# Lightweight convolution and SiLU layer on one core: exponents clamped on ScalarE, and one block's taps issued ahead of another's matmuls

## The chip, the core and the metric

One core of a Trainium2 chip runs the whole program. The metric is the device time in microseconds (us); lower is better. Three runs of the kernel before give 2204.98, 2205.42 and 2208.08 us, median 2205.42. The engines are TensorE (PE; its weight loads are PEld), VectorE (DVE), ScalarE (ACT), GpSimd (POOL) and SyncE (SP, which here issues most DMAs). Each works through its own queue in order.

## What is computed

`x` is 8 x 4096 x 192 (32768 rows of 192 channels), fp32. `weight` is 8 x 7; `w_in` is 192 x 2048, `w_out` 2048 x 192.

```python
w = softmax(weight, axis=-1)                  # 8 heads x 7 taps, each head has 24 channels
x_pad = 6 rows of zeros ahead of each of the 8 sequences
y[b, s, h, g] = sum_k w[h, k] * x_pad[b, s + k, h, g]
h = y.reshape(32768, 192) @ w_in
g = h * (1 / (1 + exp(-h)))
out = g @ w_out                               # float32
```

## The kernel before

**Blocks.** The 32768 rows go in 32 blocks of 1024 (`TT`). For each block: x is loaded (`load`, token `ld`), transposed on VectorE (`turn_in`, `i`), given a halo of six columns (`halo_in`, `ha`), and the seven taps are applied (`conv`, `v`): tap 0 on ScalarE, taps 1 to 6 as one multiply-add each on VectorE. Each block has a wide part of 1024 columns (`v.00` to `v.06`) and a narrow one of 512 (`v.10` to `v.16`). The result is split into a high part (`hx`), a low part (`lx`) and a difference (`dx`, moved by DMA in `dm`). Then come the h matmuls (`up`, tokens A, B, C, E), a scaling in place (X), the Silu on ScalarE (S), sums of g on VectorE (`s..`), and the down projection of the *previous* block (Q, D), its store (`st`).

**The order.** Nothing is left to a scheduler: `pin` keeps every engine's instructions in the order in which the program issues them, and from block 1 on that order is the string `PLAN` (lines 63 to 87), walked by the loop at line 852. A token with `-` belongs to the block before, one with `+` to the next; `step` (614) issues a token once and skips it ever after. Token T (line 518) is a copy of one column of a PSUM bank into the tile `dot` on VectorE. It reads the second bank of a pair of h banks, so the next matmul that writes this bank must wait for it. In `PLAN`, `C.00 A.000 T.00 A.010 C.01 T.01 A.001`: A.001 writes the bank that T.00 reads.

**The weights.** The inputs `w_in` and `w_out` come as 64-bit words and are rounded to fp32 in integer arithmetic. That is a `Unit` (line 306): units 0 to 7 are `w_in` (part 0, 512 columns, and part 1, 256 columns, for each of four j), units 8 to 11 are `w_out` (768 columns). For a unit,

- `exponent` masks the exponent bits on VectorE, then clamps and rescales them in two operations, on VectorE for units 0 and 8 (`late` is false there) and on GpSimd for the other ten;
- `sign` (ScalarE) turns the lowest byte into a sticky bit; `mantissa` and `sticky` are VectorE;
- `rounded` is three VectorE operations: the first needs mantissa and sticky, the second the clamped exponent, the third writes the weights to `wd`;
- `top` (ScalarE) makes the high part; `split` makes a low part with a subtraction on VectorE, copies it on ScalarE and makes a third part on VectorE. The low part stands in one buffer for all units of part 0 and one for all of part 1;
- `spread` sends halves of part 1 to the other 64 partitions by DMA.

`begin` (649) issues exponent and sign; `work` (655) is a generator of two pieces: begin of the next unit, mantissa and sticky; then rounded, top and spread.

**Block 0** (lines 762 to 839) runs on plain fp32 while the weights become ready. TensorE convolves its 128 first channels itself (`conv_on_pe`), ScalarE copies the four results (`conv_taken`) to `x_first[0]`; the other 64 channels are convolved by `conv(0, 1, i)`. `up_both(0)` and `up_first(j, c0)` are its h matmuls, each ended by four Silus on ScalarE for a set of four banks; `up_first` takes 128-row matmuls in one turn and 64-row ones in the other. The first h matmul needs unit 0, the first 64-row one needs unit 1 and all taps, `j` needs units 2j and 2j + 1. `woven` (676) interleaves these with the pieces of units 2 to 9 by hand-given costs, which decides the order in ScalarE's queue. Around the up matmuls that order reads: sign 7, top 6, four Silus, copy of split 2, sign 8, top 7, four Silus, copies of splits 5, 4, 7, 6.

Behind them (lines 812 to 831): loads of block 1, units 10 and 11, block 1's transposes, eight of the sums in `combine_out`, its taps, its high and low parts, block 2's loads, block 1's differences, block 2's transposes. Then block 0's plain down projection on TensorE (192 matmuls), and the loop over `PLAN` from block 1 on, in which block 2's taps stand as `+v..` between block 1's matmuls.

Of the kernel before, what the change touches and what calls it, by code (L numbers as in the profile page):

```python
# [8 lines left out]
F32 = mybir.dt.float32  # L9
# [3 lines left out]
AF = mybir.ActivationFunctionType  # L13
ALU = mybir.AluOpType
# [4 lines left out]
def kernel(  # L19
# [18 lines left out]
    H, K = weight.shape  # L38
    NT = B * S
    DFF = moe_w_in.shape[1]  # L40
    P = 128
# [8 lines left out]
    NJ = NCH // 4  # L50
    SQ = 32
    HT = TB // 2
    SPLIT = 4096.0
    assert D == NK * R == H * grp and NK == 3 and S % TT == 0 and DFF == 4 * P * NJ

    x_w = x.flatten_outer_dims().rearrange("(b k t) d -> b t k d", k=TT // SQ, t=SQ)
# [3 lines left out]
    const = ctx.enter_context(tc.tile_pool(name="const", bufs=1))  # L60
# [74 lines left out]
    class Pinned:  # L135
        def __init__(self, engine):
            self.engine = engine
# [4 lines left out]
    vec, act, pool = Pinned(nc.vector), Pinned(nc.scalar), Pinned(nc.gpsimd)  # L142
    sync = Pinned(nc.sync)

    def flat(t):
        names = "abcd"[: len(t.shape) - 1]
        return t.rearrange(f"p {' '.join(names)} -> p ({' '.join(names)})")
# [4 lines left out]
    def f32(t):  # L152
        return t.bitcast(F32)
# [63 lines left out]

    NG = D // SQ
    room = flat(g_all[:, 0, 0])
    used = [0]  # L220

    def early(n):
        used[0] += n
        return room[:, used[0] - n : used[0]]

    w32 = early(SQ)
# [16 lines left out]
    warm = early(1)  # L243
    vec.memset(zeros, 0.0)
    vec.memset(warm, 0.0)
    act.activation(warm, warm, AF.Exp)

    one_hot = early(R)
# [30 lines left out]
    def raw(key):  # L279
        if RAW[key] is None:  # L280
            return flat(g_all[:, 1, 8:11]).bitcast(I32)[:, WC : 3 * WC]
        return flat(RAW[key]).bitcast(I32)[:, 0 : 2 * WC]
# [10 lines left out]
    def load_out(q, queue):  # L293
        queue.dma_start(out=raw(("o", q)).rearrange("p (c d) -> p c d", c=4), in_=out32[q])
# [2 lines left out]
    LOW = CA + CB  # L297
    spare = flat(g_all[:, 1, 8:11])
    low_all, sticky_out = spare[:, 0:LOW], spare[:, LOW + 2 * WC : 2 * LOW + 2 * WC]
    ONE = 1 << 20  # L300
    NEW_SLOTS = 8
    BELOW = 1.0 - 2.0**-13

# [2 lines left out]
    class Unit:  # L306


        def __init__(self, index, key, part):
            j = key[1]  # L310
            self.key, self.part, self.j, self.late = key, part, j, index > 0
            lo, hi = {0: (0, CA), 1: (CA, WC), None: (0, WC)}[part]
            n = hi - lo
            words = raw(key)[:, 2 * lo : 2 * hi]
            pairs = words.rearrange("p (c t) -> p c t", t=2)
            self.lo, self.hi = pairs[:, :, 0], pairs[:, :, 1]
            self.byte = words.bitcast(U8).rearrange("p (c t) -> p c t", t=8)[:, :, 0]
            at_ = scratch[:, 2 * WC * (index % 2) : 2 * WC * (index % 2) + 2 * WC]
            self.ex = at_[:, 0:n].bitcast(I32)
            self.mh = at_[:, n : 2 * n].bitcast(I32)  # L320
            if part is None:
                self.w = wd[:, j, 0:12, :].rearrange("p (a s) d -> p (a s d)", a=2)
                self.st = sticky_out.bitcast(I32)
            else:
                self.low = low_all[:, CA * part : CA * part + n]
                self.st = self.low.bitcast(I32)
            if part is not None:
                at_c = slice(0, 4) if part == 0 else slice(0, 2)
                self.to = [flat(w[:, j, at_c, :]) for w in ws[part]]
                self.w = flat(w_in[part][:, j, at_c, :])  # L330

        def exponent(self):
            vec.tensor_single_scalar(self.ex, self.hi, 0x7FF * ONE, op=ALU.bitwise_and)
            engine = pool if self.late else vec
            engine.tensor_scalar(
                self.ex, self.ex, scalar1=float(896 * ONE), scalar2=float(1151 * ONE), op0=ALU.max, op1=ALU.min
            )
            engine.tensor_scalar(
                self.ex, self.ex, scalar1=float(896 * ONE), scalar2=8.0, op0=ALU.subtract, op1=ALU.mult
            )  # L340

        def sign(self):
            act.activation(self.st, self.byte, AF.Sign)
# [1 line left out]
        def mantissa(self):  # L345
            vec.tensor_scalar(
                self.mh, self.hi, scalar1=ONE - 1, scalar2=ONE, op0=ALU.bitwise_and, op1=ALU.bitwise_or
            )
# [21 lines left out]
        def split(self):  # L370
            vec.tensor_tensor(self.low, self.w, f32(self.to[0]), op=ALU.subtract)
            act.activation(self.to[1], self.low, AF.Copy, scale=SPLIT)
            vec.scalar_tensor_tensor(
                out=self.to[2], in0=f32(self.to[0]), scalar=1.0 / SPLIT, in1=self.low, op0=ALU.mult, op1=ALU.subtract
            )
# [20 lines left out]
    def heat(times):  # L396
        for _ in range(times):
            pin(
                nc.tensor.matmul(
                    banks[5][:, 0 : 2 * P],  # L400
                    zeros,
                    zeros.unsqueeze(1).to_broadcast([P, 2, P]),
                    start=True,
                    stop=True,
                )
            )
# [11 lines left out]
    by_channel = early(D)  # L418
    top, total, part_ = (wred[:, i : i + 1] for i in range(3))
    heat(7)  # L420
    for q in range(1, 4):
        vec.tensor_copy(w32[SQ * q : SQ * q + H, 0:K], w32[0:H, 0:K])
    vec.tensor_reduce(top, logits, axis=AX.X, op=ALU.max, negate=True)
    act.activation(logits, logits, AF.Exp, bias=top, accum_out=total)
    for i in (1, 3):
# [39 lines left out]
    def conv(b, k, i):  # L465
        n = (TT, TB)[k]
        src, dst, tap = xts[k][:, i : i + n], flat(nats[k]), taps[:, k, i : i + 1]
        if i == 0:
            act.activation(dst, src, AF.Copy, scale=tap)
        else:  # L470
            vec.scalar_tensor_tensor(
                out=dst, in0=src, scalar=tap, in1=dst, op0=ALU.mult, op1=ALU.add
            )

    def split(b, k, what):
# [6 lines left out]
        else:  # L482
            vec.scalar_tensor_tensor(
                out=di if k else d_room(b), in0=f32(lo), scalar=SPLIT, in1=f32(hi), op0=ALU.mult, op1=ALU.subtract
            )

    def d_room(b):

        return flat(g_all[:, 1, 8]) if b == 1 else flat(nats[0])
# [12 lines left out]
    def up(b, what, j, c, n=0):  # L502
# [16 lines left out]
        elif what == "X":  # L519
            to = at(b, names[n])  # L520
            if f"X.{j}{c}{n}" in ON_DVE:
                vec.tensor_scalar(to, to, scalar1=1.0 + 1.0 / SPLIT, scalar2=None, op0=ALU.mult)
            else:
                act.activation(to, to, AF.Copy, scale=1.0 + 1.0 / SPLIT)
        else:
# [118 lines left out]
    units = [Unit(2 * j + i, ("i", j), i) for j in range(NJ) for i in range(2)]  # L644
# [4 lines left out]
    def begin(u):  # L649
        if u < len(units):  # L650
            units[u].exponent()
            if u <= 2 * NJ:
                units[u].sign()

    def work(u):

        now = units[u]
        if u > 1:
            begin(u + 1)
        now.mantissa()  # L660
        now.sticky()
        if 2 * NJ < u + 1 < len(units):
            units[u + 1].sign()
        yield
        if not u:
            begin(1)
        now.rounded()
        if now.part is not None:
            if u:
                now.top()  # L670
            now.spread(w_in[1][:, now.j, :, :])
        if u in LATER:
            load_out(LATER[u], sync)
        yield
# [33 lines left out]
    def conv_taken(q):  # L708
        act.copy(x_first[0][:, ts(q, HT)], banks[q][:, 0:HT])

    def drain(stream):
        for _ in stream:
            pass

    def pieces(stream, *costs):
        def one():
            next(stream, None)

        return [(one, cost) for cost in costs]

    def pieces_of_work(u):
        return pieces(work(u), *((26, 30) if u >= 2 * NJ else (14, 13) if u % 2 else (16, 21)))

    x_first = [flat(nats[k]) for k in range(2)]

# [42 lines left out]
    turn_first(True)  # L768
    conv_on_pe(1)
    begin(0)  # L770
    first_ = [work(u) for u in range(2)]
    next(first_[0])
    for q in (0, 2):
# [3 lines left out]
    for q in range(4):  # L777
        at_ = slice(SQ * q, SQ * q + SQ)
        pool.tensor_copy(taps[at_, 1, :], taps_all[at_, 4 + q % 2, 0:K])
        pool.tensor_copy(taps[at_, 0, :], taps_all[at_, ORDER[q], 0:K])  # L780
    conv(0, 1, 0)
    next(first_[0])
    for q in (1, 3):
        conv_taken(q)
    units[0].top()
    conv(0, 1, 1)
    for stream in first_:
        drain(stream)
    begin(2)
    for i in range(2, K):  # L790
        conv(0, 1, i)
    for part in (0, 1):
        load_in(3, part, sync)
# [4 lines left out]
    turns = ["ha.0", "i.0", "ha.1", "i.1", "ha.2"]  # L798
    convs = [t for t in rest_of if t.split(".")[0] == "v"]
    rest = []  # L800
    SPLIT_AFTER = {3: (1,), 4: (0,), 5: (3,), 6: (2,), 7: (5, 4, 7, 6)}
    for u in range(2, 2 * NJ):
        rest += pieces_of_work(u)
        rest += [(units[v].split, 8 if v % 2 else 14) for v in SPLIT_AFTER.get(u, ())]
    for u in (2 * NJ, 2 * NJ + 1):
        rest += pieces_of_work(u)
# [7 lines left out]
    for u in (2 * NJ + 2, 2 * NJ + 3):  # L814
        drain(work(u))
# [8 lines left out]
        step(2, t)  # L824
    for t in ("dx.0", "dx.1", "dm.0"):
        step(1, t)
    for t in turns:
        step(2, t)
    for t in plan:
        if t[0] == "*":  # L830
# [21 lines left out]
    for b in range(1, NB + 3):  # L852
        for t in plan:
            if b == 2 and t[:2] == "-Q":
                drain(late)
            name = t[1:] if t[0] in BACK else t
# [44 lines left out]
```

## Time and profile before

| what | us |
|---|---|
| median of three runs (lowest, highest) | 2205.42 (2204.98, 2208.08) |
| the profiled execution, device time | 2204.53 |
| its span, first to last instruction | 2202.7 |
| TensorE busy in the span | 2192.1 |
| VectorE, ScalarE, GpSimd busy | 1868.1, 1218.8, 52.3 |
| first h matmul of block 0, of block 1, of block 2 starts at | 14.37, 99.93, 169.46 |

The granted TensorE clock is 0.999 over the span. Times of rows below count from the first instruction. A timeline row gives start, length, engine, line, operation, out<-in, the shape and how many instructions were merged in it; in brackets, the idle time of the engine before it and what ended it. Nearly all instructions carry line 140 (the wrapper that pins them), matmuls line 498, so the tiles tell what a row is: `wd` takes rounded weights, `nat` with `taps` is a tap, `xt<-nat` a transpose, `dot` is token T, `g<-ps` a Silu, `xs` the split parts of x.

### The profile page before, as it was taken

How to read it: one execution, taken by the hardware profiler on the slowest of the kernel's cores; microseconds unless marked ns; L12 is line 12 of the kernel's file. 1: busy time of each engine (PE TensorE's matmuls, PEld its weight loads, DVE VectorE, ACT ScalarE, POOL GpSimd, SP SyncE). 2: the span in 40 equal slices, each digit the busy share in tenths (PEclk: the TensorE clock that was granted, in tenths of full speed). 3: DMA queues.
4: the chain of work that ended last, by engine and by line, in shares of the span. 5: the costliest groups of instructions: out<-in, count | busy, mean ns of one | idle time of the engine just before them, and what ended most of it. 6: DMA issues, size and time to landing. Idle time of an engine off the chain costs nothing.

```text
span 2202.7 us, 46351 instructions
## 1 busy us (share of the span) xinstructions
PE 2192.1 (100%) x19294; PEld 1585.3 (72%) x19294; DVE 1868.1 (85%) x2723; ACT 1218.8 (55%) x2457; POOL 52.3 (2%) x75
## 2 busy tenths in 40 slices
PE   9999999999999999999999999999999999999998
PEld 4477777777777777777777777777777777777776
DVE  8898888888888888888888888888888888888867
ACT  5356654466544566545665446664456654466543
POOL 4300000000000000000000000000000000000000
PEclk9999999999999999999999999999999999999999
DMA  6412022220122210222201222112222022221112
GB/s 160 80 25 36 7 37 39 40 39 15 26 39 39 39 30 11 39 40 40 39 13 28 39 39 39 24 17 40 39 39 38 8 34 40 40 39 20 21 25 49
DMA packets 416579, 80.10 MB, mean 36 GB/s; under 512 B 402544, under 2 KB 406640, under 8 KB 416368
## 3 DMA queue, kind: packets, MB, share of 16 engines
q1 hardware_dynamic: 411760, 75.42, 18.7%
q8 instruction: 151, 2.47, 0.5%
q0 software_dynamic: 288, 1.05, 0.3%
q10 hardware_dynamic: 4320, 0.66, 0.2%
q14 instruction: 60, 0.49, 0.1%
HBM read 31.47 MB, written 25.17 MB: 26 GB/s over the span
## 4 chain that ended last, share of the span: by engine, by line
PE 95%; DVE 1%; SPq 0%; ACT 0%; issue 0%; DMA 0%; DVEq 0%
PE ps L498 95%; DVE nat L140 1%; SPq L140 0%; DVE wd L140 0%; DVE fin L140 0%; DMA xs<-g 0%; DVE xt L140 0%; ACT nat L140 0%; ACT fin L140 0%; DVE xs L140 0%; ACT ps L140 0%; DVEq L140 0%; DVE dot L140 0%
## 5 line engine op out<-in xcount | busy, mean ns | idle before, releaser
L498 PE MATMUL ps<-g,wd 128*64 128x256 f32 (+1 forms) x10112 | 1118.8, 383 | 0.0
L498 PEld LDWEIGHTS ps<-g,wd 128*64 128x64 f32 x10112 | 723.5, 137 | 392.0 <-issue 26.7
L140 DVE TENSOR_TENSOR g<-g 128x1024 f32<-128x1024 f32 (+1 forms) x811 | 945.5, 1210 | 21.2 <-PE ps L498 11.3
L140 ACT ACTIVATE ps<-ps 128x512 f32<-128x512 f32 (+1 forms) x961 | 499.4, 581 | 421.7 <-PE ps L498 387.3
L140 ACT ACTIVATE g<-ps 128x512 f32<-128x512 f32 x1024 | 557.6, 631 | 32.9 <-PE ps L498 32.3
L498 PE MATMUL ps<-xs,w_a 64*128 64x512 f32 x3968 | 566.8, 386 | 0.4 <-DVE dot L140 0.4
L498 PE MATMUL ps<-xs,w_b 64*128 64x512 f32 x2976 | 488.6, 389 | 0.4 <-ACT ps L140 0.4
L498 PEld LDWEIGHTS ps<-xs,w_a 64*128 64x128 f32 x3968 | 372.5, 184 | 79.1 <-DVE dot L140 1.0
L140 DVE SCALAR_TENSOR_TENSOR nat<-xt,taps,nat 128x512 f32<-128x512 f32 (+1 forms) x378 | 373.5, 1001 | 2.6
L498 PEld LDWEIGHTS ps<-xs,w_b 64*128 64x128 f32 x2976 | 277.4, 184 | 69.4 <-issue 12.4
L498 PE MATMUL ps<-xs,w_d 64*128 64x512 f32 x1984 | 321.4, 386 | 0.0
L140 DVE COPY dot<-ps 128x1 f32<-128x1 f32 x496 | 78.1, 157 | 247.7 <-PE ps L498 238.9
L498 PEld LDWEIGHTS ps<-xs,w_d 64*128 64x128 f32 x1984 | 186.6, 184 | 38.6
L140 ACT ACTIVATE fin<-ps 128x256 f32<-128x256 f32 x93 | 35.8, 385 | 206.5 <-PE ps L498 206.5
L140 DVE TENSOR_SCALAR ps<-ps 128x512 f32<-128x512 f32 x124 | 86.4, 697 | 34.7 <-PE ps L498 34.7
L140 ACT ACTIVATE nat<-xt,taps 128x512 f32<-128x512 f32 (+1 forms) x63 | 58.6, 934 | 80.8 <-DVE xt L140 79.4
L140 ACT COPY fin<-ps 128x256 f32<-128x256 f32 (+1 forms) x127 | 41.6, 380 | 108.1 <-PE ps L498 108.1
L140 DVE TENSOR_TENSOR fin<-fin,ps 128x256 f32<-128x256 f32 x248 | 96.4, 408 | 0.8 <-PE ps L498 0.8
L140 DVE STREAM_TRANSPOSE fin<-fin 128x256 f32<-128x256 f32 (+1 forms) x189 | 82.9, 440 | 0.4 <-ACT fin L140 0.2
L140 DVE STREAM_TRANSPOSE xt<-nat 128x1024 f32<-128x1024 f32 (+3 forms) x67 | 62.4, 935 | 3.1 <-DMA nat<-in_x_dram 3.1
L140 ACT ACTIVATE xs<-nat 128x1024 fp32r<-128x1024 f32 (+1 forms) x62 | 52.3, 843 | 12.3 <-DVE nat L140 12.3
L140 DVE TENSOR_TENSOR xs<-nat,xs 128x1024 fp32r<-128x1024 f32 (+1 forms) x62 | 58.7, 947 | 0.0
(52 smaller groups left out, 362.1 us busy)
## 6 DMA issues: line engine op xcount, KB each, us to landing
out_dram<-fin SPq DMA_DIRECT2D x242, 96.0 KB, 2.7
nat<-in_x_dram SPq DMA_DIRECT2D x124, 128.0 KB, 3.1
xs<-nat SPq DMA_DIRECT2D x120, 128.0 KB, 2.3
nat<-in_x_dram SPq DMA_DIRECT2D x131, 64.0 KB, 2.7
g<-in_moe_w_in_dram SPq DMA_DIRECT2D x12, 128.0 KB, 3.2
fin<-in_moe_w_in_dram SPq DMA_DIRECT2D x12, 128.0 KB, 3.1
g<-in_moe_w_out_dram SPq DMA_DIRECT2D x2, 768.0 KB, 5.1
w_b<-w_b SPq DMA_DIRECT2D x8, 192.0 KB, 4.1
```

The lines of the kernel that those rows point to most:

```text
L140: return lambda *args, **kw: pin(getattr(self.engine, name)(*args, **kw))
L498: return pin(nc.tensor.matmul(to, lhs, rhs, start=start, stop=True, skip_group_check=True))
```

## The change

- Every unit's clamp goes to ScalarE: two Relu activations whose bias is one of two constants in a new tile `ends`, set by two memsets at the start. VectorE keeps the mask. The flag `late` goes.
- Unit 1's sign moves ahead of unit 0's rounding; its mask and clamp move behind that rounding and the last `conv_taken`.
- Unit 2's `begin` moves from ahead of the taps 2 to 6 of block 0's 64 channels to between taps 3 and 4.
- One of three small copies of `weight` goes from VectorE to GpSimd.
- The costs given to `woven` change; the order that comes out on ScalarE is otherwise as before.
- Block 2's taps `v.00` to `v.06` and `v.10` to `v.13` are issued right behind its transposes, ahead of block 0's down projection and of block 1's plan; `v.14` to `v.16` stay in the plan.

```diff
+    ends = const.tile([P, 2], F32, name="ends")
...
+    for i, end in enumerate((1151 * ONE, 8 * 255 * ONE)):
+        vec.memset(ends[:, i : i + 1], float(end))
...
         def exponent(self):
             vec.tensor_single_scalar(self.ex, self.hi, 0x7FF * ONE, op=ALU.bitwise_and)
-            engine = pool if self.late else vec
-            engine.tensor_scalar(
-                self.ex, self.ex, scalar1=float(896 * ONE), scalar2=float(1151 * ONE), op0=ALU.max, op1=ALU.min
-            )
-            engine.tensor_scalar(
-                self.ex, self.ex, scalar1=float(896 * ONE), scalar2=8.0, op0=ALU.subtract, op1=ALU.mult
-            )
+
+        def clamp(self):
+
+            act.activation(self.ex.bitcast(F32), self.ex, AF.Relu, bias=ends[:, 0:1], scale=-1.0)
+            act.activation(self.ex, self.ex.bitcast(F32), AF.Relu, bias=ends[:, 1:2], scale=-8.0)
...
-    for q in range(1, 4):
-        vec.tensor_copy(w32[SQ * q : SQ * q + H, 0:K], w32[0:H, 0:K])
+    for q, copy in enumerate((vec.tensor_copy, vec.tensor_copy, pool.tensor_copy)):
+        copy(w32[SQ * q + SQ : SQ * q + SQ + H, 0:K], w32[0:H, 0:K])
...
             units[u].exponent()
             if u <= 2 * NJ:
                 units[u].sign()
+            units[u].clamp()
...
-        if not u:
-            begin(1)
         now.rounded()
...
-        return pieces(work(u), *((26, 30) if u >= 2 * NJ else (14, 13) if u % 2 else (16, 21)))
+        return pieces(work(u), *((20, 29) if u >= 2 * NJ else (10, 13) if u % 2 else (15, 21)))
...
     conv(0, 1, 0)
+    units[1].sign()
     next(first_[0])
     for q in (1, 3):
         conv_taken(q)
+    units[1].exponent()
+    units[1].clamp()
     units[0].top()
     conv(0, 1, 1)
     for stream in first_:
         drain(stream)
-    begin(2)
     for i in range(2, K):
+        if i == K - 3:
+            begin(2)
         conv(0, 1, i)
...
-    for t in turns:
+    for t in (*turns, *(t for t in convs if t not in ("v.14", "v.15", "v.16"))):
         step(2, t)
```

More of the change, by code (lines that the diff above doesn't have):

```diff
@@ L53 @@
     SPLIT = 4096.0
+    ONE = 1 << 20
     assert D == NK * R == H * grp and NK == 3 and S % TT == 0 and DFF == 4 * P * NJ
@@ L299 @@
     low_all, sticky_out = spare[:, 0:LOW], spare[:, LOW + 2 * WC : 2 * LOW + 2 * WC]
-    ONE = 1 << 20
     NEW_SLOTS = 8
@@ L310, in __init__ @@
             j = key[1]
-            self.key, self.part, self.j, self.late = key, part, j, index > 0
+            self.key, self.part, self.j = key, part, j
             lo, hi = {0: (0, CA), 1: (CA, WC), None: (0, WC)}[part]
```

## The prediction

> **What bounds the kernel now.** I read the page first, then TensorE in order of time, then what ended each of its waits.
>
> ```profile
> span 2202.7 us, 46351 instructions
> PE 2192.1 (100%) x19294; PEld 1585.3 (72%) x19294; DVE 1868.1 (85%) x2723; ACT 1218.8 (55%) x2457; POOL 52.3 (2%) x75
> PE ps L498 95%; DVE nat L140 1%; SPq L140 0%; DVE wd L140 0%; DVE fin L140 0%; DMA xs<-g 0%; DVE xt L140 0%; ACT nat L140 0%; ACT fin L140 0%; DVE xs L140 0%; ACT ps L140 0%; DVEq L140 0%; DVE dot L140 0%
> ```
>
> TensorE is never without work, so only its gaps count. The timeline of PE (start, length, instruction, idle before it in brackets):
>
> ```profile
> 14.37 7.11 PE L498 MATMUL ps<-nat,wd 128*128 128x512 f32 x16 [1.56 <-DMA g<-in_moe_w_in_dram]
> 99.93 0.73 PE L498 MATMUL ps<-xs,w_b 64*128 64x512 f32 x4
> 101.87 0.62 PE L498 MATMUL ps<-xs,w_a 64*128 64x512 f32 x4
> 104.72 0.98 PE L498 MATMUL ps<-xs,w_b 64*128 64x512 f32 x2 [0.42 <-ACT ps L140]
> 112.94 0.73 PE L498 MATMUL ps<-xs,w_a 64*128 64x512 f32 x4 [0.42 <-DVE dot L140]
> 134.77 5.40 PE L498 MATMUL ps<-g,wd 128*64 128x256 f32 x48
> 169.46 0.73 PE L498 MATMUL ps<-xs,w_b 64*128 64x512 f32 x4
> 202.32 0.87 PE L498 MATMUL ps<-g,wd 128*64 128x256 f32 x6
> ```
>
> Block 0 multiplies from 14.37 to 99.93. Block 1's h takes 134.77 - 99.93 = 34.84 us, block 2's 202.32 - 169.46 = 32.86: 1.98 us are lost, all behind 101.87. What comes later the change doesn't touch. Inside block 0 the weight loads show two gaps:
>
> ```profile
> 21.70 0.37 PEld L498 LDWEIGHTS ps<-nat,wd 64*128 64x128 f32 x4 [1.06 <-DVE nat L140]
> 29.04 0.29 PEld L498 LDWEIGHTS ps<-nat,wd 64*128 64x128 f32 x2 [0.76 <-DVE g L140]
> 29.92 0.30 PEld L498 LDWEIGHTS ps<-nat,wd 64*128 64x128 f32 x4 [0.59 <-DMA wd<-wd]
> 33.55 0.30 PEld L498 LDWEIGHTS ps<-nat,wd 128*128 128x128 f32 x2 [0.76 <-issue]
> 51.31 0.30 PEld L498 LDWEIGHTS ps<-nat,wd 64*128 64x128 f32 x4 [0.76 <-DVE g L140]
> 54.95 0.30 PEld L498 LDWEIGHTS ps<-nat,wd 128*128 128x128 f32 x2 [0.76 <-issue]
> ```
>
> A change of shape costs 0.76 anyway, so 21.70 waited 1.06 - 0.76 = 0.30 us for the taps. The stretch 29.04 to 33.55 takes 4.51 where 51.31 to 54.95 takes 3.64: 0.87 us behind unit 3's DMA. Together 1.17.
>
> **The change, part by part.** *Start.* Unit 0's weights now come thus:
>
> ```profile
> 8.32 1.64 DVE L140 TENSOR_SCALAR g<-g 128x512 int32<-128x512 int32 x4
> 11.49 0.72 ACT L140 ACTIVATE nat<-xt,taps 128x512 f32<-128x512 f32 x1
> 11.74 0.30 DVE L140 TENSOR_SCALAR g<-g 128x256 int32<-128x256 int32 x1 [0.56 <-DMA g<-in_moe_w_in_dram]
> 12.87 0.65 ACT L140 COPY nat<-ps 128x256 f32<-128x256 f32 x2 [0.31 <-PE ps L498]
> 13.47 0.69 DVE L140 SCALAR_TENSOR_TENSOR wd<-g 128x512 f32<-128x512 f32 x1
> 17.10 4.55 DVE L140 SCALAR_TENSOR_TENSOR nat<-xt,taps,nat 128x512 f32<-128x512 f32 x5
> ```
>
> The weights are written at 13.47 + 0.69 = 14.16, the first matmul starts at 14.37. Two of the four VectorE operations at 8.32 go (2 x 0.41 = 0.8), and unit 1's mask leaves the path with its wait (0.56 + 0.2). The weights would stand at 12.6. The two clamps on ScalarE, priced like the one activation here with a pointer operand (0.72), take 1.45 behind the sign and lie beside mantissa, sticky and transpose. Now ScalarE's copy at 12.87 is late: it waits for TensorE's own convolution. Its first half ends near 13.24, so the first matmul starts near 13.4: 0.97 won. The third copy of w32 on GpSimd and the two small memsets lie beside a wait for the weight's DMA: -0.1 to +0.1, I take 0.
>
> *The 1.17 inside block 0.* Unit 0's two operations and unit 1's wait (1.4) go, and GpSimd beside the five taps at 17.10 (0.91 each; the narrow taps in the row of 79.67 below come every 0.79): 0.6. So the taps end 2.0 sooner and TensorE wants them 0.97 sooner: the 0.30 goes. Unit 3 must come 0.97 + 0.30 + 0.87 = 2.1 sooner for its 0.87 to go whole. It has the 2.0, and GpSimd goes from beside units 2 and 3 too, so I count all of 1.17 (at the worst 0.3 stay). Block 1's h could begin at 99.93 - 0.97 - 1.17 = 97.8.
>
> *Where ScalarE takes the place of GpSimd.* GpSimd's 20 clamps (ten units) held up VectorE alone. On ScalarE 24 stand in one queue with the Silus, the signs and the copies, and VectorE waits for that queue:
>
> ```profile
> 36.43 1.57 ACT L140 ACTIVATE g<-ps 128x512 f32<-128x512 f32 x3 [1.12 <-PE ps L498]
> 44.25 0.30 PEld L498 LDWEIGHTS ps<-nat,wd 128*128 128x128 f32 x2 [0.76 <-issue]
> 45.28 0.95 ACT L140 ACTIVATE g<-g 128x768 int32<-128x768 uint8 x1
> 47.42 2.04 ACT L140 ACTIVATE g<-ps 128x512 f32<-128x512 f32 x4
> 49.32 0.44 ACT L140 ACTIVATE w_b<-g 128x256 fp32r<-128x256 f32 x1
> 49.79 0.42 DVE L140 TENSOR_TENSOR g<-wd,w_b 128x256 f32<-128x256 f32 x1 [0.61 <-ACT w_b L140]
> 51.92 0.55 DVE L140 TENSOR_SCALAR g<-fin 128x768 int32<-128x768 int32 x1
> ```
>
> At 49.79 VectorE waits until ScalarE has copied unit 5's low part (same buffer), and ScalarE copies it behind the four Silus of 47.42. These need TensorE: its group starts at 44.25, 2.14 earlier in the new order, 42.1; by the pattern of 33.55 and 36.43 (2.88 to the second Silu) the Silus could run from 45.0, be done at 46.5 and the copy at 46.9. That is the earliest. But ScalarE, from 34.3 (36.43 less 2.14) on without a pause, has 11 Silus (2.04 for four: 5.6), four signs, copies and tops 512 wide (as a Silu, 0.51 each: 2.0), five 256 wide (0.44, less 0.1 of overlap: 1.7), one sign 768 wide (0.95 less 0.1) and, new, the clamps of units 6, 7 and 8: 1.45, 1.0 and 1.9, from the 0.72 by width. That is 14.5, and the copy ends at 48.8. I take **48.7**, only 1.1 before the 49.79 of now; between 46.9 and 49.8 all is open. VectorE can't get past this wait, however much is taken from it.
>
> *From there to block 1, all on VectorE.*
>
> ```profile
> 70.77 0.55 DVE L140 TENSOR_SCALAR g<-g 128x768 int32<-128x768 int32 x1
> 74.14 0.96 DVE L140 SCALAR_TENSOR_TENSOR wd<-g 128x768 f32<-128x768 f32 x1
> 79.67 12.48 DVE L140 SCALAR_TENSOR_TENSOR nat<-xt,taps,nat 128x1024 f32<-128x1024 f32 x12
> 92.07 1.82 DVE L140 TENSOR_TENSOR xs<-nat,xs 128x1024 fp32r<-128x1024 f32 x2
> 98.20 1.25 DVE L140 STREAM_TRANSPOSE xt<-nat 128x1024 f32<-128x1024 f32 x1 [2.58 <-DMA nat<-in_x_dram]
> 99.99 0.71 DVE L140 STREAM_TRANSPOSE xt<-nat 128x512 f32<-128x512 f32 x1 [0.54 <-DMA nat<-in_x_dram]
> 102.39 1.79 ACT L140 ACTIVATE nat<-xt,taps 128x512 f32<-128x512 f32 x2
> 101.17 0.16 DVE L140 COPY dot<-ps 128x1 f32<-128x1 f32 x1 [0.47 <-PE ps L498]
> ```
>
> Splits of 7 and 6: 51.92 - 49.79 = 2.1. Units 8 to 11: unit 11 ran with no GpSimd beside it, 70.77 to 75.10, 4.33; four of these and three masks of 0.47 are 18.7. So 20.8 to the end of unit 11 (now 25.3). From 75.10 to the first low part of block 1 (92.07 + 1.2 = 93.28) 18.2, as now. That store frees the buffer for block 2's loads; the transposes, behind the loads, end 7.4 later (100.70), as now.
>
> Here stands the last edit. Block 2's taps are issued between those transposes and T.00, the one-column copy at 101.17 that matmul A.001 (101.87) must wait for. Two taps of ScalarE come first (the wide one 1.15, the 1.79 of 102.39 is both): 1.4 with the halo copy. Then VectorE's six wide (1.31) and three narrow (0.79): 10.3. T.00 comes 7.4 + 1.4 + 10.3 = 19.1 behind the store that frees the buffer, where it now comes 7.9 behind.
>
> The sum: 48.7 + 20.8 + 18.2 + 19.1 = 106.8 for T.00, 107.0 for A.001, where TensorE is there at 97.8 + 1.94 = 99.7 and stands for **7.3 us**. Everything won before is spent in this wait: what counts is A.001's delay, 107.0 - 101.87 = +5.1. Behind it VectorE has ten fewer us of taps in block 1 and ScalarE two fewer activations ahead of its scalings: the 1.98 goes, -2.0.
>
> *TensorE behind a long wait.* The first matmuls of the program, windows of them alone:
>
> ```profile
> 1.00:5.00 4.00, 3.90 (x9) 3.16 (x10) 1.00 0.62 158
> 5.00:6.50 1.50, 1.42 (x6) 0.83 (x5) 1.00 1.08 249
> ```
>
> 9 in 4.0 us, then 6 in 1.5, of one shape: about half rate for 4.0 us behind idleness, although the granted clock reads 1.00. Behind the idle 1.56 before 14.37 no such phase shows (16 in 7.11, 0.44 each, the usual pace). A stand of 7 us lies above this; the same phase would cost half of 4.0, 2.0. Its bounds are 0 and 3.6 (half rate for as long as the stand). I take 2.0, the one row that shows TensorE after a long rest.
>
> The Trainium skill, "TensorE: Matmul & The Clock Gate", part 1, says that an idle window of about 3.4 us halves the array's clock until a busy window has passed. By this page the phase would cost about 1.7, an estimate, in place of 2.0; the two windows above agree with it in kind, and no row shows it in mid-kernel.
>
> Result: 5.1 - 2.0 + 2.0 = +5.1 on the profiled execution's own 2204.53 (its span and 1.8 around it): 2209.6. The median of the three runs, 2205.42, is 0.9 above that execution, so I give **2210.5**.
>
> **Rivals.** (1) *T.00 comes in time*: VectorE isn't held by ScalarE's copy. For it: VectorE is busy nearly throughout, so what leaves it could carry it far ahead. Against: the bracket at 49.79 names ScalarE, and the Silus ahead of that copy can't precede TensorE. It decides at T.00 before 99.5, which needs the copy at 99.5 - 58.1 = 41.4, 8.4 before now. Then the gains stay, -0.97 - 1.17 - 2.0 = -4.1: 2201.3, and 2202.3 with a wait of 1.
> (2) *The wait, but no slow phase*: +3.1, 2208.5; with the copy at its earliest, 46.9 in place of 48.7, +1.3, 2206.7. For it: no row shows the phase but at the start.
> (3) *ScalarE costs more*: clamps at twice the 0.72 would push the copy 4.3 further, to 53: +9, 2215. Against it: the sign of 45.28 reads integers and takes 0.95 at 768, what 0.72 at 512 gives there.
> (4) *Relu isn't in the loaded table*: each clamp pair would need a load before and after it, and a load couldn't be had for less than an activation, 0.72: 24 of them are 17 us on ScalarE's path, 2222 or more. Sign, Copy and Silu already share one table here.
>
> The Trainium skill, "ScalarE: Activation LUTs", rules for kernel authors, would leave relu-like work on VectorE. By it the clamps would cost VectorE 0.8 per wide unit, and T.00 would come later still.
>
> **How the numbers follow.** Forecast (wait and slow phase; 2209 to 2213) 0.52, (1) 0.18, (2) 0.20, (3) 0.08, (4) 0.02. About 0.2% (4.4 us) is what a measurement of this kernel tells from no change: under 2201.0 faster, over 2209.8 slower. Slower: 0.38 of the forecast's 0.52, and (3) and (4): 0.48. Faster: the better end of (1), 0.08. Same: 0.44. The range takes in (1), (2), the forecast and the cheaper half of (3): 2201 to 2214. That leaves out about 0.1.
>
> **What would show it.** Right: the first matmul near 13.4; no GpSimd clamps; block 1's first h near 97.8; VectorE's dot first at 105 to 108 with taps straight before it; a PE row with 5 to 8 us of idle "<-DVE dot"; matmuls behind it at half pace; block 1's h otherwise 32.9. Wrong: dot before 100 and no such row, or a table load between Silus.

## The result, and the profile after

The changed kernel takes 2209.70 us (median of 20 runs, 2209.06 to 2211.07) against 2204.87 for the kernel before, run beside it (median of 20): 4.8 us more, ratio 1.002, 95% interval 1.0014 to 1.0026. The prediction was 2210.5, 5.1 above the median it started from. The profiled execution's span grows from 2202.7 to 2207.8. Of all executions below, one, of e3, ran at a granted clock of 0.85 and took 2493.49 us; it stands in no ratio.

TensorE in order of time, in the changed kernel (start, length, what, how many; in brackets the idle time before and what ended it; lines have moved by one, matmuls are L499):

```profile
13.28 43.03 PE L499 MATMUL ps<-nat,wd 128*128 128x512 f32 x128 [0.52 <-ACT nat L141]
56.24 41.42 PE L499 MATMUL ps<-g,wd 128*64 128x512 f32 x192
97.59 0.74 PE L499 MATMUL ps<-xs,w_b 64*128 64x512 f32 x4
99.10 0.63 PE L499 MATMUL ps<-xs,w_b 64*128 64x512 f32 x4
106.86 1.22 PE L499 MATMUL ps<-xs,w_a 64*128 64x512 f32 x4 [7.13 <-DVE dot L141]
139.88 1.30 PE L499 MATMUL ps<-g,wd 128*64 128x256 f32 x10
174.57 0.74 PE L499 MATMUL ps<-xs,w_b 64*128 64x512 f32 x4
207.47 0.87 PE L499 MATMUL ps<-g,wd 128*64 128x256 f32 x6
```

Block 0 starts at 13.28 (14.37 before) and runs without a gap: its matmuls stand in one row up to the down projection. Block 1's h starts at 97.59 (99.93 before), so 2.34 us are won. Then TensorE stands for 7.13 us until VectorE's `dot`, token T.00. Block 1's h takes 139.88 - 97.59 = 42.29; block 2's 207.47 - 174.57 = 32.90, as before.

What VectorE and ScalarE did (the engine stands behind the length in each row):

```profile
34.09 1.57 ACT L141 ACTIVATE g<-ps 128x512 f32<-128x512 f32 x3 [0.57 <-PE ps L499]
34.15 0.62 DVE L141 TENSOR_SCALAR g<-fin 128x256 int32<-128x256 int32 x2
36.93 0.70 DVE L141 SCALAR_TENSOR_TENSOR fin<-fin,g 128x512 int32<-128x512 int32 x1 [2.16 <-ACT g L141]
43.96 1.91 ACT L141 ACTIVATE g<-g,ends 128x768 f32<-128x768 int32 x2
47.99 0.43 ACT L141 ACTIVATE w_b<-g 128x256 fp32r<-128x256 f32 x1
48.45 0.43 DVE L141 TENSOR_TENSOR g<-wd,w_b 128x256 f32<-128x256 f32 x1 [3.01 <-ACT w_b L141]
68.47 0.96 DVE L141 SCALAR_TENSOR_TENSOR wd<-g 128x768 f32<-128x768 f32 x1
86.39 1.82 DVE L141 TENSOR_TENSOR xs<-nat,xs 128x1024 fp32r<-128x1024 f32 x2
93.04 1.25 DVE L141 STREAM_TRANSPOSE xt<-nat 128x1024 f32<-128x1024 f32 x1 [3.09 <-DMA nat<-in_x_dram]
96.61 10.12 DVE L141 SCALAR_TENSOR_TENSOR nat<-xt,taps,nat 128x1024 f32<-128x1024 f32 x9 [1.44 <-ACT nat L141]
106.66 0.15 DVE L141 COPY dot<-ps 128x1 f32<-128x1 f32 x1
```

VectorE now waits for ScalarE twice for long: 2.16 us for unit 6's sign, and 3.01 at the sub (the subtraction in `split`) of unit 7, for ScalarE's copy of 47.99; three waits ahead of these are 0.28 to 0.52 each. Its sub starts at 48.45 where it started at 49.79. The nine taps of block 2 are one unbroken row from 96.61 to the copy at 106.66 that TensorE waits for.

TensorE's own windows around the wait (us, busy and number of matmuls, of weight loads, granted clock, then DMA):

```profile
99.80:104.20 4.40, 0.00 (x0) 0.00 (x0) 1.00 0.00 0
104.30:106.80 2.50, 0.00 (x0) 0.00 (x0) 0.50 0.00 0
106.90:111.00 4.10, 4.10 (x20) 3.26 (x22) 0.50 0.37 64
111.10:113.10 2.00, 2.00 (x20) 1.61 (x20) 1.00 0.69 117
```

The granted clock falls to 0.50 during the wait and stays there for 4.1 us of matmuls: 20 in 4.1 us, then 20 in 2.0.

The sum: -1.09 at the start, -1.25 in block 0, then block 1's h, 42.29 in place of 34.84, +7.45: +5.1, which is the span's 2207.8 - 2202.7. Of the 42.29, 32.86 is an undisturbed stage; A.001 comes at 106.86, 7.33 behind the 97.59 + 1.94 at which TensorE wanted it; 2.1 is left for the slow phase.

### The profile page after: what moved, and what is told of

Read it like the earlier page. It is cut to its first block, busy times and chain, and to the rows that moved or that the text cites. A ratio compares the mean times of both kernels' runs of the same rounds, so it can differ in the third digit from the quotient of the medians.

```text
span 2207.8 us, 46355 instructions
## 1 busy us (share of the span) xinstructions
PE 2192.2 (99%) x19294; PEld 1585.4 (72%) x19294; DVE 1858.1 (84%) x2720; ACT 1234.7 (56%) x2481; POOL 11.7 (1%) x56
## 4 chain that ended last, share of the span: by engine, by line
PE 95%; DVE 1%; SPq 0%; issue 0%; DMA 0%; ACT 0%; DVEq 0%
PE ps L499 95%; DVE nat L141 1%; SPq L141 0%; DVE fin L141 0%; DVE wd L141 0%; DMA xs<-g 0%; DVE xt L141 0%; DVE xs L141 0%; ACT nat L141 0%; ACT fin L141 0%; DVEq L141 0%; DVE dot L141 0%
## 5 line engine op out<-in xcount | busy, mean ns | idle before, releaser
L499 PE MATMUL ps<-g,wd 128*64 128x256 f32 (+1 forms) x10112 | 1118.8, 383 | 0.0
L499 PEld LDWEIGHTS ps<-g,wd 128*64 128x64 f32 x10112 | 723.5, 137 | 392.0 <-issue 27.3
L499 PE MATMUL ps<-xs,w_a 64*128 64x512 f32 x3968 | 567.5, 387 | 7.1 <-DVE dot L141 7.1
L499 PE MATMUL ps<-xs,w_b 64*128 64x512 f32 x2976 | 488.3, 389 | 0.0
L499 PEld LDWEIGHTS ps<-xs,w_a 64*128 64x128 f32 x3968 | 372.8, 184 | 86.1 <-DVE dot L141 7.6
L499 PEld LDWEIGHTS ps<-xs,w_b 64*128 64x128 f32 x2976 | 277.3, 184 | 68.6 <-issue 11.5
L499 PE MATMUL ps<-xs,w_d 64*128 64x512 f32 x1984 | 320.8, 386 | 0.0
L499 PEld LDWEIGHTS ps<-xs,w_d 64*128 64x128 f32 x1984 | 186.0, 184 | 38.8
```

The costliest lines, as they stand in the source:

```text
L499: return pin(nc.tensor.matmul(to, lhs, rhs, start=start, stop=True, skip_group_check=True))
```

## The experiments

Theory: the taps ahead of T.00 alone make TensorE wait, since ScalarE's queue keeps VectorE from running ahead, and idleness itself slows the matmuls behind. The rivals stand with each run. All kernels do the reference's whole work; e4 has 30 matmuls more. Ratios are to the kernel before on the same chip, with 95% intervals.

**e1, clamps alone:** the last edit undone.

```diff
-    for t in (*turns, *(t for t in convs if t not in ("v.14", "v.15", "v.16"))):
+    for t in turns:
```

> The clamps on ScalarE without the last edit: block 2's taps stand in the plan again, as before the change. Theory (the taps ahead of T.00 alone make the wait, the clamps only gain): T.00 comes in time, no wait of 7 us and no slow phase; block 1's h begins at 97.6 as in the changed kernel and takes 34.8 or a little less, so about 2202.5 us, 2.3 under before. Rival (the load that the clamps put on ScalarE is what costs): part of the 4.8 us stays, 2206 to 2210.

Measured: 2201.33, ratio 0.9983 (0.9975 to 0.9992). In this kernel:

```profile
97.64 0.73 PE L499 MATMUL ps<-xs,w_b 64*128 64x512 f32 x4
98.87 0.16 DVE L141 COPY dot<-ps 128x1 f32<-128x1 f32 x1 [3.59 <-PE ps L499]
109.47 0.73 PE L499 MATMUL ps<-xs,w_a 64*128 64x512 f32 x4 [0.43 <-DVE dot L141]
131.28 1.08 PE L499 MATMUL ps<-g,wd 128*64 128x256 f32 x8
```

T.00 comes at 98.87, with VectorE idle ahead of it; one of block 1's two 0.4 us gaps is left. Block 1's h takes 131.28 - 97.64 = 33.64, where I allowed 34.8 at most: with VectorE 5 us further on, 1.2 of the 2.0 are gone without any tap ahead. The clamps with the new order at the start only gain; the rival falls.

**e2, taps alone:** the last edit on the kernel before.

```diff
-    for t in turns:
+    for t in (*turns, *(t for t in convs if t not in ("v.14", "v.15", "v.16"))):
```

> The last edit alone, on the kernel before: block 2's taps ahead of block 1's h, clamps on VectorE and GpSimd as before. Theory: the first low part of block 1 stands at 93.3 as before, T.00 19.1 behind it at 112.4, TensorE is there at 101.9: a wait of 10.7 us, then a slow phase of 2, and block 1's 2 us of small gaps go: +10.8, about 2215.7. Rival (VectorE has room for the taps in the 5 us that it idles around block 1's start, and the wait came from the clamps on ScalarE): within 1 of before, 2204 to 2206.

Measured: 2214.96, ratio 1.0046 (1.0031 to 1.0062).

```profile
101.97 10.13 DVE L140 SCALAR_TENSOR_TENSOR nat<-xt,taps,nat 128x1024 f32<-128x1024 f32 x9 [1.44 <-ACT nat L140]
112.01 0.15 DVE L140 COPY dot<-ps 128x1 f32<-128x1 f32 x1
112.22 1.22 PE L498 MATMUL ps<-xs,w_a 64*128 64x512 f32 x4 [10.23 <-DVE dot L140]
```

The same nine taps, the same order, 5.4 us later: TensorE waits 10.23, where 10.7 was expected. Taps and clamps aren't independent: the clamps take 3.1 off the wait. VectorE's idle time at block 1's start was no room for taps; most of it is the wait for block 2's loads, which the taps need.

**e3, two taps ahead** in place of nine on VectorE.

```diff
-    for t in (*turns, *(t for t in convs if t not in ("v.14", "v.15", "v.16"))):
+    for t in (*turns, *("v.00", "v.01", "v.02", "v.10",)):
```

> The changed kernel with fewer taps ahead: v.00 and v.10 (ScalarE) and v.01, v.02 (VectorE, 1.32 each); the other seven go back into the plan. Theory: v.01 starts at 96.6, T.00 comes at 99.3, TensorE needs it at 99.5: no wait. The 2.3 of the start stay and ScalarE's two taps no longer stand ahead of its scalings, so up to 2 more: 2200.5 to 2202, less than both kernels. Rival (any taps ahead of T.00 make TensorE wait, for the loads of block 2 or for ScalarE's taps): a wait of 1 to 3 us, 2203 to 2205.

Measured: 2200.29, ratio 0.9981 (0.9972 to 0.9990), the least of all, 4.1 under the kernel before, where the changed one is 4.8 over it.

```profile
96.31 2.61 DVE L141 SCALAR_TENSOR_TENSOR nat<-xt,taps,nat 128x1024 f32<-128x1024 f32 x2 [1.44 <-ACT nat L141]
98.83 0.16 DVE L141 COPY dot<-ps 128x1 f32<-128x1 f32 x1
97.60 0.73 PE L499 MATMUL ps<-xs,w_b 64*128 64x512 f32 x4
99.55 0.62 PE L499 MATMUL ps<-xs,w_a 64*128 64x512 f32 x4
130.48 0.87 PE L499 MATMUL ps<-g,wd 128*64 128x256 f32 x6
```

T.00 comes at 98.83, 0.7 before A.001 is due, and A.001 follows at 99.55 without a bracket. Block 1's h takes 32.88, an undisturbed stage. e1 and e3 lie within each other's intervals; their medians differ by 1.0, their profiles by 0.76 in this stage.

**e4, TensorE kept busy in the wait.**

```diff
+            if b == 1 and t == "A.001":
+                for _ in range(30):
+                    pin(nc.tensor.matmul(homes[0], w_b[:, 0, 0, 0, :], xs[1][:, 0, :], start=True, stop=True, skip_group_check=True))
```

> The changed kernel with 30 more matmuls of 128 x 512 ahead of A.001, into a bank whose content is overwritten right after; they add nothing to the result. They fill some 6.5 of the 7.3 us that TensorE stands. Theory (the slow matmuls behind the wait come from the idleness itself): A.001 comes at the same time, 106.9, but the matmuls behind it run at the full pace: 2.1 less than the changed kernel, 2207.6. Rival (they are slow because of what the wait leaves behind, banks to be freed or VectorE and ScalarE catching up): still half pace behind A.001, 2209.7.

Measured: 2207.33, ratio 1.0012 (1.0003 to 1.0022).

```profile
99.61 7.12 PE L863 MATMUL ps<-xs,w_b 128*128 128x512 f32 x30
106.66 0.73 PE L499 MATMUL ps<-xs,w_a 64*128 64x512 f32 x4
106.70:110.70 4.00, 4.00 (x36) 3.29 (x38) 1.00 0.48 82
```

A.001 comes at 106.66, no sooner to speak of, but behind it 36 matmuls run in 4.0 us at a granted clock of 1.00. The slow phase comes from the idleness and not from anything that stood in a queue: it costs 1.9 by the medians (4.83 over the kernel before, here 2.94), 2.1 by the sum above.

**e5, VectorE let past its wait for ScalarE:** the splits of units 7 and 6 behind unit 8.

```diff
-    SPLIT_AFTER = {3: (1,), 4: (0,), 5: (3,), 6: (2,), 7: (5, 4, 7, 6)}
+    SPLIT_AFTER = {3: (1,), 4: (0,), 5: (3,), 6: (2,), 7: (5, 4), 8: (7, 6)}
...
         rest += pieces_of_work(u)
+        rest += [(units[v].split, 8 if v % 2 else 14) for v in SPLIT_AFTER.get(u, ())]
```

> The changed kernel with the splits of units 7 and 6 issued behind unit 8 in place of ahead of it; nothing is left out. Theory (VectorE stands 3.0 us at the sub of unit 7, because ScalarE's copy of unit 5 stands behind clamps and Silus, and this alone sets when T.00 comes): VectorE does unit 8 in that time, T.00 comes 3.0 sooner at 103.7, TensorE waits 4.2 in place of 7.1: 2206.5 with a slow phase behind the wait, 2204.6 without one. Rival (VectorE's own work is the bound and the 3.0 only moves to another place in its queue): T.00 at 106.7, 2209.5.

Measured: 2205.73, ratio 1.0006 (0.9997 to 1.0015).

```profile
45.21 0.55 DVE L141 TENSOR_SCALAR g<-fin 128x768 int32<-128x768 int32 x1
49.94 0.42 DVE L141 TENSOR_TENSOR g<-wd,w_b 128x256 f32<-128x256 f32 x1
103.47 0.15 DVE L141 COPY dot<-ps 128x1 f32<-128x1 f32 x1
103.68 0.85 PE L499 MATMUL ps<-xs,w_a 64*128 64x512 f32 x4 [4.13 <-DVE dot L141]
```

Unit 8 fills the 3.01; T.00 comes 3.2 sooner, and so does A.001. The copy on ScalarE does set T.00, and the 3 us don't come back elsewhere. But a wait of 4.13 is left: ScalarE's queue sets how long the wait is, and the taps alone would make one.

**e8 and e6, four and five wide taps ahead:** the line of e3 with `"v.00", "v.01", "v.02", "v.03", "v.04", "v.10"`, and with `"v.05"` too.

> The changed kernel with v.01 to v.04 ahead (v.00 and v.10 on ScalarE too). Theory: T.00 at 96.4 + 4 x 1.31 = 101.7, TensorE stands 2.4 us and, by what a rest of 1.6 ahead of the first h matmul shows, comes back at full pace: 2202.7. Rival (a rest of 2.4 is enough for the slow phase): 2204.7.

> The changed kernel with v.01 to v.05 ahead (v.00 and v.10 on ScalarE too), v.06 and the narrow ones in the plan. Theory (each wide tap ahead puts T.00 off by 1.31): T.00 at 96.4 + 5 x 1.31 = 103.0, TensorE stands 3.7 us: 2200.3 + 3.7 = 2204.0 if it comes back at full pace, 2206 if a rest of 3.7 already brings the slow phase. Rival (the wait isn't made of taps one by one): as the changed kernel, 2209.5.

Measured: e8 2202.75, ratio 0.9994 (0.9984 to 1.0003); e6 2205.33, ratio 1.0003 (0.9994 to 1.0012). The waits, e8's first:

```profile
102.02 0.74 PE L499 MATMUL ps<-xs,w_a 64*128 64x512 f32 x4 [2.26 <-DVE dot L141]
102.10:106.10 4.00, 4.00 (x36) 3.27 (x38) 1.00 0.31 54
```

```profile
103.79 0.72 PE L499 MATMUL ps<-xs,w_a 64*128 64x512 f32 x4 [3.72 <-DVE dot L141]
103.80:105.20 1.40, 1.40 (x12) 1.19 (x14) 1.00 0.04 12
105.30:108.60 3.30, 3.30 (x18) 2.62 (x16) 0.50 0.56 95
```

The wait is made of taps one by one. Behind 2.26 us the clock stays in the profiled execution; behind 3.72 it falls, but only 1.4 us after TensorE is back at work. It doesn't fall every time: of e6's ten executions the three with a mean granted clock of 1.000 took 2203.91 to 2204.58, the five with 0.998 took 2205.49 to 2206.96. So e6's median lies between the 2204.0 of full pace and the 2206 of the slow phase. Of e8's ten, four took 2203.69 to 2204.45 and the others 2202.14 to 2202.92; the profiled one is of the six, so whether the clock fell in the four isn't shown.

**e7, GpSimd keeps the late clamps:** e1 with the clamps of all units but 0 and 1 on GpSimd, as two operations each.

```diff
         def clamp(self):
+            if self.key != ("i", 0):
+                pool.tensor_scalar(
+                    self.ex, self.ex, scalar1=float(896 * ONE), scalar2=float(1151 * ONE), op0=ALU.max, op1=ALU.min
+                )
+                pool.tensor_scalar(
+                    self.ex, self.ex, scalar1=float(896 * ONE), scalar2=8.0, op0=ALU.subtract, op1=ALU.mult
+                )
+                return
```

> The kernel of the clamps alone, but only units 0 and 1 have them on ScalarE; GpSimd does the other ten. Theory (the start and the order there win the 2.3 ahead of block 1, and ScalarE's clamps of the late units only carry VectorE further ahead): block 1's h begins at 97.6 to 98.0 as with all clamps on ScalarE; VectorE comes to it 4 to 5 us later, so block 1's h takes 34.0 to 34.8 in place of 33.6: 2201.7 to 2202.8. Rival (taking GpSimd off VectorE is what wins): the gaps at unit 3 and at the taps come back, block 1's h begins at 98.7 or later, 2203 to 2204.

Measured: 2201.91, ratio 0.9987 (0.9978 to 0.9995).

```profile
27.48 0.29 PEld L507 LDWEIGHTS ps<-nat,wd 64*128 64x128 f32 x2 [0.76 <-DVE g L141]
31.64 0.30 PEld L507 LDWEIGHTS ps<-nat,wd 128*128 128x128 f32 x2 [0.76 <-issue]
47.12 0.43 DVE L141 TENSOR_TENSOR g<-wd,w_b 128x256 f32<-128x256 f32 x1 [0.24 <-ACT w_b L141]
98.02 0.73 PE L507 MATMUL ps<-xs,w_b 64*128 64x512 f32 x4
132.05 0.65 PE L507 MATMUL ps<-g,wd 128*64 128x256 f32 x4
```

Unit 3's stretch takes 4.16 in place of 3.64, so 0.5 of its gap is back; block 1's h starts at 98.0 and takes 34.0. In the profiles this comes to 0.8 against e1, in the medians to 0.6, which their intervals don't part. So 1.9 of the 2.3 us ahead of block 1 come from the order at the start together with two units' clamps on ScalarE; no run parts these two. This run also shows what held VectorE: with the late clamps off ScalarE, its wait at the sub of unit 7 is 0.24 in place of the changed kernel's 3.01.

## Why the prediction held, step by step

- **Start.** Predicted 13.4, came 13.28, and the bracket names ScalarE's copy (`nat`), as said. Unit 0's weights stood at 12.30, where 12.6 was said; the copy hides this. GpSimd's third copy and the memsets were put at nothing: TensorE's convolution starts 0.06 earlier.
- **Block 0's gaps.** Predicted 1.17, came 1.25: all of it. What came better than said here and at the start, 0.2, only made the wait longer and can't show in the total.
- **ScalarE's queue.** The copy that VectorE waits for was put at an end of 48.7 (46.9 at the earliest); it ended at 48.42. ScalarE was to work from 34.3 on for 14.5 us without a pause; it did so from 34.09 for 14.33. The clamp pair at 768 was priced at 1.9 and took 1.91. This step made the size: VectorE lost 2.16 and 3.01 us in waits, where it had waited 0.61 before. The sign hung on it less: e5, without the 3.01, is still 1.35 over the kernel before, though its interval includes no change at all.
- **VectorE's chain.** From its sub to T.00: 20.8 + 18.2 + 19.1 = 58.1 predicted, 106.66 - 48.45 = 58.2 measured, in parts 21.0, 18.2 and 19.0. T.00 was put at 106.8.
- **The wait.** 7.3 predicted, 7.33 measured.
- **The slow phase.** 2.0 taken, 2.1 measured; e4 shows that it is a step of its own. That there is one was argued from the first matmuls of the program, though their granted clock reads 1.00 and the one behind the wait reads 0.50. That the size agrees to 0.1 is luck: rests of 3.7 to 10.2 us cost between nothing (some executions of e6, by their times) and 2.8 (e2) besides their length.
- **Block 1's gaps.** The 2.0 went as said, but e1 shows that 1.2 of it needs no tap ahead; two taps ahead, which make no wait, are worth the other 0.8 (e3).
- **Rivals.** (1), T.00 in time, didn't come with nine taps; e3 reaches it with two: 4.1 under the kernel before, as was given for it. (2), no slow phase, is what e4 makes: 2.9 over, for 3.1. Nothing came of (3), the clamps cost what was said, or of (4): ScalarE's two table loads stand at the start, as before.
- **The number.** 2210.5 is 0.8 too high. The profiled executions differ by 2209.54 - 2204.53 = 5.0, for 5.1 in the sum. Most of the 0.8 is the median that it was added to: 2205.42 of three runs, where twenty give 2204.87.

## What to carry to other kernels

Work moved ahead in an engine's queue is ahead of everything that stands behind it there, however small: here 10 us of taps stood before a one-column copy on which TensorE waited, and two taps fitted where nine did not. How early VectorE came was set by its last wait for another engine, not by the work taken from it; look for such a wait in the brackets and count from there. A stand of TensorE can cost more than its length: 1.7 to 2.8 us more in the profiled executions with rests of 3.7 us and above.

## What the runs showed of the hardware

TensorE's clock falls in steps that don't start with its rest. In e5 the rest is over before the clock falls:

```profile
99.60:103.60 4.00, 0.00 (x0) 0.00 (x0) 1.00 0.00 0
103.70:104.10 0.40, 0.40 (x4) 0.36 (x6) 1.00 0.00 0
104.20:107.50 3.30, 3.30 (x18) 2.54 (x18) 0.50 0.35 62
107.60:109.60 2.00, 2.00 (x20) 1.64 (x20) 1.00 0.69 119
```

It is halved for some 3.4 us, in e6 as well; in the changed kernel for some 6.8 (104.2 to 111.1), and in e2, with a rest of 10.23, for 13.6:

```profile
102.00:104.10 2.10, 0.00 (x0) 0.00 (x0) 1.00 0.01 1
104.20:112.20 8.00, 0.00 (x0) 0.00 (x0) 0.50 0.00 0
112.30:117.80 5.50, 5.50 (x26) 4.38 (x28) 0.50 0.36 61
```

Here it fell some 2.2 us into the rest, so the 2.26 of e8 isn't shown to be safe in every run. The Trainium skill, "TensorE: Matmul & The Clock Gate", part 1, says that the clock is judged in windows of about 3.4 us that run freely and don't reset when a kernel starts: one, two and four of them fit these lengths. The page lets the clock fall after an idle window; in e6 TensorE had been back at work for 1.4 us when it fell, so a window need not be idle throughout, or the fall comes late, and no run here tells which. Besides its own length a rest cost half of what ran slowly behind it: 1.7 us in e5 and e6, 2.1 in the changed kernel, 2.8 in e2, and by the times of e6 nothing where the clock stayed.
